# Sliding-window attention and a gated unit on one core: loads by units of four heads, square transposes, and scores issued half a pair ahead

## The chip, the cores and the metric

The kernel runs on one core of a Trainium2 chip. The core has TensorE (PE in the profile; PEld is its weight loads), VectorE (DVE), ScalarE (ACT), GpSimd (POOL) and SyncE (SP), and 16 DMA engines that SP, ACT and POOL hand transfers to. Each engine works through its own instructions in program order and waits on semaphores. The metric is the device time in microseconds, the median of several runs; lower is better.

## What is computed

```python
def _attn_ref(q, k, v):                       # (8, 8, 576, 64) each, float32
    window, dilation, scale = 32, 4, 1.0 / np.sqrt(D)
    scores = scale * np.matmul(q, k.transpose(0, 1, 3, 2))
    rel = pos[:, None] - pos[None, :]
    mask_plain = (rel >= 0) & (rel < window)
    mask_dil = (rel >= 0) & (rel < window * dilation) & (rel % dilation == 0)
    masks = [mask_plain if h < H // 2 else mask_dil for h in range(H)]
    ...                                       # masked softmax over keys
    return np.matmul(attn, v)
def _moe_ref(x, w_val, conv_w, w_out):        # x: heads joined, (8, 576, 512)
    ...                                       # causal, 5 taps per channel
        gate_pre += conv_w[k][None, None, :] * xp[:, k:k + S, :]
    gate = 1.0 / (1.0 + np.exp(-gate_pre))
    return (gate * (x @ w_val)) @ w_out       # (8, 576, 512) float32
```

## The kernel before

The kernel works on 32 pairs of heads (8 batches, 4 pairs each; pairs 0 and 1 are plain, 2 and 3 dilated). The program order of every engine is the order in which the Python code issues; nothing is rescheduled. Positions are split in four residue classes r = position mod 4 with 144 members each; a dilated head is a plain window of 32 inside each class.

*Loads.* `load_qk(i)` and `load_v(i)` fetch one pair, all on SP's queue. A partition takes four neighbouring positions of a head, a row of 1 KB; as 144 partitions do not fit, each tensor comes as a tile of 96 (`qa`, `ka`, `va`) and one of 48 rows (`qzd`/`kzd` for dilated, `qzp`/`kzp` for plain pairs; `vz` has 80). Plain v comes in rows of 256 bytes (`vp`), in six overlapping chunks of 128 keys. `convert(i)` casts on POOL: v of dilated pairs (L136), q and k of plain pairs (L143). Pair i+2 is loaded and cast while pair i runs.

*Attention of a pair.* `transpose_in` turns q and k to head-dimension-major with TensorE (L161 and L163 for dilated, L167 and L171 for plain pairs), in transposes of 96 and 48 rows; DVE copies the result out (L182), ACT for k of plain pairs (L179). `scores(i, hf)`, hf being a half of the pair, multiplies k by q for two heads side by side, 64 rows of the array each (L197), into one of two score tiles `sc` in PSUM; exp on ACT (L212) and the mask on DVE (L219) give `et`. Dilated classes are cut in 96 and 48 queries. `attn_v(i, hf)` multiplies `et` with v (L236, L240 dilated, L246 plain), writes into the same score tile, and DVE divides by the sum (reciprocal L251, product into `xn` L256). `transpose_x` turns `xn` back (L269, L271 by turns for dilated; L275 plain), and ACT copies it into `xT` (L278).

*Gated unit.* It works on groups of 512 tokens (the last ones of 448, 320 and 256). For each of four channel blocks there is a unit C (conv as five diagonal matmuls, L303, tanh on ACT, L307) and a unit V (product with w_val, L315, gating on DVE into `y_all`, L320); for each 128 tokens a unit O (product with w_out, L329, copy out on ACT, L332, output DMA from ACT's queue, L333). These units, the transposes and the copies share four PSUM banks (`bank`). Units of a batch become available when its four pairs are done. They wait in a queue, and `fill(share)` issues units as long as a budget lasts, so that they lie between the steps of the attention:

```python
    per = 3.2
    for i in range(n_steps):
        ...                        # load_qk, load_v, convert of pair i + 2
        scores(i, 0)
        scores(i, 1)
        fill(per * 0.35)
        attn_v(i, 0)
        if i + 1 < n_steps:
            transpose_in(i + 1, "q")
            transpose_in(i + 1, "k")
        attn_v(i, 1)
        fill(per * 0.65)
        transpose_x(i)
```

What is left in the queue after the last pair is issued at the end.

## Time and profile before

| | |
|---|---|
| median of three runs | 228.96 us (226.93 to 231.23) |
| the profiled execution | 225.51 us, of which the span of the profile is 223.8 us |
| mean granted TensorE clock | 0.992 |
| DMA | 41.82 MB in 58757 packets, mean 187 GB/s |

The page's first part has the busy time of each engine, its share of the span and its instructions; the second cuts the span into 40 slices of 5.6 us, a digit being a busy share in tenths:

```profile
PE 189.1 (85%) x2279; PEld 127.0 (57%) x2292; DVE 128.4 (57%) x311; ACT 108.7 (49%) x190; POOL 65.0 (29%) x123
...
PE   2666689878988898898898898889888988999992
...
DVE  2566664775667556663666659656776566532320
ACT  2234444356554655475544753465536654643442
...
DMA  5799999747779799869989779778986300221232
GB/s 144 240 220 207 236 216 225 211 120 232 213 212 231 234 254 224 217 222 258 233 192 243 234 217 237 181 244 227 232 213 212 118 3 0 99 91 47 100 141 94
```

And some of its groups (line, engine, operation, output and input, shape, count, then busy us, mean ns of one, and the idle time before them):

```profile
L256 DVE TENSOR_TENSOR xn<-sc,rec 96x512 bf16<-96x512 f32 (+1 forms) x64 | 39.7, 620 | 2.2
L212 ACT ACTIVATE et<-sc 128x576 bf16<-128x576 f32 x64 | 38.5, 660 | 4.8 <-PE sc L197 4.8
L332 ACT ACTIVATE osb<-bank 128x512 f32<-128x512 f32 x36 | 21.6, 601 | 29.4 <-PE bank L329 23.4
L179 ACT COPY kT<-bank 128x576 bf16<-128x576 bf16 x16 | 10.2, 638 | 20.4 <-PE bank L171 16.4
L182 DVE COPY qT<-bank 128x576 bf16<-128x576 bf16 x32 | 14.2, 444 | 3.3 <-PE bank L163 3.0
```

A busy TensorE is not one at its peak: the end of a matmul is modelled, and an isolated one of 65 columns counts some 200 ns.

### The profile page before, as it was taken

Reading aid. Unit: us, or ns where it says so; the run is one execution under the profiler, and the core shown is the slowest. Engines: PE = TensorE matmul, PEld = TensorE weight load, DVE = VectorE, ACT = ScalarE, POOL = GpSimd, SP = SyncE. Lnnn points to the kernel's source line nnn. Section 1 sums busy time; section 2 is a strip of 40 time slices with the busy share of each in tenths; the row PEclk is TensorE's granted clock in tenths of the full one; section 3 lists DMA queues with packets and bytes.
Section 4 is the critical chain, followed back from the end, with each engine's and each line's share of the span. In section 5 each row is a group of like instructions: output and inputs, shape, how many; then the busy total and the mean of one; then the engine's idle time right before and its main releaser. Section 6 shows DMA issues by size and latency. Waiting matters only on the chain.

```text
span 223.8 us, 5850 instructions
## 1 busy us (share of the span) xinstructions
PE 189.1 (85%) x2279; PEld 127.0 (57%) x2292; DVE 128.4 (57%) x311; ACT 108.7 (49%) x190; POOL 65.0 (29%) x123
## 2 busy tenths in 40 slices
PE   2666689878988898898898898889888988999992
PEld 0544545545655576556775686558655666454670
DVE  2566664775667556663666659656776566532320
ACT  2234444356554655475544753465536654643442
POOL 4296506420516150524146024602360200000000
PEclk9999999999999999996999999999999999999999
DMA  5799999747779799869989779778986300221232
GB/s 144 240 220 207 236 216 225 211 120 232 213 212 231 234 254 224 217 222 258 233 192 243 234 217 237 181 244 227 232 213 212 118 3 0 99 91 47 100 141 94
DMA packets 58757, 41.82 MB, mean 187 GB/s; under 512 B 29029, under 2 KB 54117, under 8 KB 58730
## 3 DMA queue, kind: packets, MB, share of 16 engines
q1 hardware_dynamic: 52480, 30.95, 56.1%
q10 hardware_dynamic: 5194, 9.45, 11.8%
q0 software_dynamic: 1056, 1.05, 2.9%
q8 instruction: 18, 0.29, 0.6%
q14 instruction: 9, 0.07, 0.1%
HBM read 33.04 MB, written 9.44 MB: 190 GB/s over the span
## 4 chain that ended last, share of the span: by engine, by line
PE 45%; DMA 15%; ACT 13%; DVE 10%; issue 7%; SPq 6%; ACTq 2%; POOL 0%; DVEq 0%
PE bank L303 16%; ACT et L212 9%; PE bank L315 8%; PE bank L329 5%; DVE et L219 4%; ACT osb L332 4%; DMA qa<-in_q_dram 4%; DVE xn L256 4%; DMA vp<-in_v_dram 3%; PE bank L269 3%; PE sc L246 2%; PE bank L271 2%; DMA ka<-in_k_dram 2%; ACTq L333 2%; DMA kzd<-in_k_dram 2%
## 5 line engine op out<-in xcount | busy, mean ns | idle before, releaser
L303 PE MATMUL bank<-xT,conv_diag 128*128 128x320 bf16 (+7 forms) x319 | 46.3, 295 | 0.3 <-DMA kzd<-in_k_dram 0.3
L256 DVE TENSOR_TENSOR xn<-sc,rec 96x512 bf16<-96x512 f32 (+1 forms) x64 | 39.7, 620 | 2.2
L212 ACT ACTIVATE et<-sc 128x576 bf16<-128x576 f32 x64 | 38.5, 660 | 4.8 <-PE sc L197 4.8
L307 ACT ACTIVATE gate<-bank 128x512 bf16<-128x512 f32 (+3 forms) x40 | 22.0, 556 | 32.8 <-PE bank L303 32.8
L315 PE MATMUL bank<-xT,w_val_b 128*128 128x320 bf16 (+7 forms) x254 | 37.1, 285 | 0.3 <-issue 0.3
L136 POOL CAST vda<-va 96x512 bf16<-96x512 f32 x16 | 10.0, 622 | 92.9 <-DMA va<-in_v_dram 79.3
L332 ACT ACTIVATE osb<-bank 128x512 f32<-128x512 f32 x36 | 21.6, 601 | 29.4 <-PE bank L329 23.4
L320 DVE SCALAR_TENSOR_TENSOR y_all<-gate,bank 128x512 bf16<-128x512 bf16 (+3 forms) x40 | 25.1, 628 | 18.0 <-PE bank L315 9.1
L303 PEld LDWEIGHTS <-conv_diag 128*128 128x128 bf16 x320 | 27.8, 100 | 12.6 <-issue 1.4
L329 PE MATMUL bank<-w_out_b,y_all 128*128 128x512 bf16 x134 | 33.7, 380 | 0.8 <-DVE y_all L320 0.2
L219 DVE TENSOR_TENSOR et<-et,mask_d 128x576 bf16<-128x576 bf16 x32 | 16.7, 524 | 27.9 <-ACT et L212 26.9
L278 ACT COPY xT<-bank 128x576 bf16<-128x576 bf16 x32 | 20.4, 637 | 23.1 <-PE bank L271 17.8
L219 DVE TENSOR_TENSOR et<-et,mask_p 128x576 bf16<-128x576 bf16 x32 | 16.8, 532 | 25.6 <-ACT et L212 24.6
L315 PEld LDWEIGHTS <-w_val_b 128*128 128x128 bf16 x256 | 20.8, 97 | 8.1
L329 PEld LDWEIGHTS <-y_all 128*128 128x128 bf16 x144 | 12.8, 98 | 14.4 <-DVE y_all L320 1.8
L179 ACT COPY kT<-bank 128x576 bf16<-128x576 bf16 x16 | 10.2, 638 | 20.4 <-PE bank L171 16.4
L236 PE MATMUL sc<-vda,et 96*128 96x65 bf16 x128 | 12.2, 203 | 7.6 <-DVE et L219 3.7
L246 PE MATMUL sc<-vp,et 128*128 128x65 bf16 x192 | 12.1, 201 | 7.5 <-DVE et L219 4.2
L269 PE MATMUL bank<-ident_b,xn 96*128 96x96 bf16 x64 | 14.1, 221 | 4.4 <-DVE xn L256 4.4
L251 DVE RECIPROCAL rec<-sc 96x8 f32<-96x8 f32 (+1 forms) x64 | 12.2, 191 | 9.5 <-PE sc L246 7.7
L182 DVE COPY qT<-bank 128x576 bf16<-128x576 bf16 x32 | 14.2, 444 | 3.3 <-PE bank L163 3.0
L236 PEld LDWEIGHTS <-et 96*128 96x128 bf16 x128 | 8.1, 100 | 14.1 <-DVE et L219 13.6
(62 smaller groups left out, 243.5 us busy)
## 6 DMA issues: line engine op xcount, KB each, us to landing
out_dram<-osb ACTq DMA_DIRECT2D x36, 256.0 KB, 2.3
qa<-in_q_dram SPq DMA_DIRECT2D x32, 192.0 KB, 4.1
ka<-in_k_dram SPq DMA_DIRECT2D x32, 192.0 KB, 3.4
vp<-in_v_dram SPq DMA_DIRECT2D x32, 160.0 KB, 3.8
va<-in_v_dram SPq DMA_DIRECT2D x16, 192.0 KB, 3.6
vz<-in_v_dram SPq DMA_DIRECT2D x16, 160.0 KB, 3.8
qzd<-in_q_dram SPq DMA_DIRECT2D x32, 48.0 KB, 3.4
kzd<-in_k_dram SPq DMA_DIRECT2D x32, 48.0 KB, 3.1
```

The lines of the kernel that those rows point to most:

```text
L212: nc.scalar.activation(out=et[:, :, 0:HALF], in_=ps[:, :, 0:HALF], func=AF.Exp, scale=scale)
L219: nc.vector.tensor_tensor(out=ev, in0=ev, in1=for_mask, op=ALU.mult)
L236: nc.tensor.matmul(out=ps[:, x, hh * DA:(hh + 1) * DA], lhsT=et[0:96, x, hh * 96:hh * 96 + 128], rhs=c0[:, hh, r, :], start=True, stop=True)
L256: nc.vector.tensor_tensor(out=xo, in0=av[:, :, :, 0:D], in1=rec[:, :, 0:n, None].to_broadcast([96, 2, n, D]), op=ALU.mult)
L269: nc.tensor.transpose(out=pv[:, r, 0:96], in_=xn[:, 2 * r, :, :].rearrange("p h d -> p (h d)"), identity=ident_b[0:96, 0:96])
L278: nc.scalar.copy(out=xT[:, g, c0:c0 + S].rearrange("p (t r) -> p t r", r=R), in_=pv.rearrange("p r t -> p t r"))
L303: nc.tensor.matmul(out=ps[:, o:o + ln], lhsT=conv_diag[:, c, kk, :], rhs=xT[:, c, s:s + ln], start=(kk == 0), stop=(kk == K - 1))
L307: nc.scalar.activation(out=gate[:, 0:n], in_=ps[:, 0:n], func=AF.Tanh, scale=0.5)
L315: nc.tensor.matmul(out=ps[:, o:o + ln], lhsT=w_val_b[:, mc, c * 128:(c + 1) * 128], rhs=xT[:, mc, col:col + ln], start=(mc == 0), stop=(mc ...
L320: nc.vector.scalar_tensor_tensor(out=y_all[:, c, t0:t0 + n], in0=gate[:, 0:n], scalar=1.0, in1=ps[:, 0:n], op0=ALU.add, op1=ALU.mult)
L329: nc.tensor.matmul(out=ps[0:n, :], lhsT=y_all[:, c, t0:t0 + n], rhs=w_out_b[:, c, :], start=(c == 0), stop=(c == NCH - 1))
L332: nc.scalar.activation(out=osb[0:n, :], in_=ps[0:n, :], func=AF.Copy, scale=0.5)
```

## The change

Work is now loaded and transposed by units of two pairs (four heads): for every batch the dilated unit, then the plain one.

- Loads: q and k of a unit fill 128 partitions. A partition takes 36 neighbouring positions (9.2 KB) in a dilated unit, with q in partitions 0 to 63 and k in 64 to 127 of one tile, and 9 positions (2.3 KB) in a plain one. SP issues one half, ACT the other. v of a dilated unit comes in tiles of 128 and 48 rows, v of a plain unit in one transfer. Buffers: two units of each kind rather than four pairs.
- Transposes into q and k: 18 of 128x128 per unit (two parts of eight, one of two). DVE copies all q, ACT all k; the copies spread the columns with a step of 9.
- Dilated classes are cut in 128 and 16 queries rather than 96 and 48. The transposes back of a dilated pair are four of 128 rows, then four of 16.
- The loop runs over half-pairs: the scores of half-step j+2 are issued in half-step j, the mask of j+1 behind the product of j, the transposes back one half-step later.
- The fill spreads the units of all groups but the last two evenly over the half-steps from 9 on. Groups end in 384, 384 and 256 tokens. `y_all` becomes three rotating tiles.

```diff
-    def load_qk(i):
...
+    def load_unit(u):
+        b, d = units[u]
+        hs = slice(4 * d, 4 * d + 4)
+        t = {}
+        if d:
+            t["qk"] = inbuf.tile([128, JD * D], FP32, name="qkd")
+            for n, (src, eng) in enumerate(((q, nc.sync), (k, nc.scalar))):
+                eng.dma_start(out=t["qk"][64 * n:64 * n + 64],
+                              in_=src[b, hs].rearrange("h (p j) d -> (h p) (j d)", j=JD))
...
+            nc.sync.dma_start(out=t["va"], in_=rows[0:128])
+            nc.sync.dma_start(out=t["vz"][W:80], in_=rows[96:TT])
+        else:
+            for name, src in (("q", q), ("k", k)):
+                t[name] = inbuf.tile([128, 2, JP * D], FP32, name=f"{name}p")
+                for e, eng in enumerate((nc.sync, nc.scalar)):
+                    eng.dma_start(
+                        out=t[name][64 * e:64 * e + 64],
+                        in_=src[b, 2 * e:2 * e + 2].rearrange("h (p j) d -> p h (j d)", j=JP))
...
+    def convert_qk(u):
+        t = loaded[u]
+        for name in ("k", "q"):
+            c = work.tile([128, JP, 2, D], BF16, name=f"{name}c", bufs=2)
+            nc.gpsimd.tensor_copy(
+                c.rearrange("p j h d -> p h j d"),
+                t[name].rearrange("p h (j d) -> p h j d", j=JP))
...
+    def transpose_in(u, part):
...
+        engines = ((qT, nc.vector.tensor_copy), (kT, nc.scalar.copy))
...
+                for m in range(8):
+                    nc.tensor.transpose(out=ps[:, m * 128:(m + 1) * 128],
+                                        in_=cols(2 * m + part), identity=ident_b)
+                for n, (dst, copy) in enumerate(engines):
+                    copy(out=dst[:, part * S:(part + 1) * S].rearrange(
+                             "p (a m) -> p a m", m=9)[:, :, 0:8],
+                         in_=ps.rearrange("p (m n a) -> p n a m", m=8, n=2)[:, n])
...
+                for j in range(8):
+                    nc.tensor.transpose(out=ps[:, j * 128:(j + 1) * 128],
+                                        in_=flat(c[:, j]), identity=ident_b)
+                copy(out=dst.rearrange("p (a j) -> p a j", j=JP)[:, :, 0:8],
+                     in_=ps.rearrange("p (j a) -> p a j", j=8))
...
     def scores(i, hf):
...
-                mm(hh * 96, 96, kT[:, o:o + 128], qT[:, o:o + 96])
...
-                mm(192 + hh * 48, 48, kT[:, o + 64:o + 192], qT[:, o + 96:o + TT])
...
+                mm(hh * 128, 128, W + o, o)
...
+                mm(256 + hh * X1, X1, W + o + 64, o + 128)
...
+    def masks(i, hf):
...
+        nc.vector.tensor_tensor(out=ev, in0=ev, in1=m, op=ALU.mult)
...
             for r in range(R):
-                nc.tensor.transpose(out=pv[:, r, 0:96], in_=xn[:, 2 * r, :, :].rearrange("p h d -> p (h d)"),
-                                    identity=ident_b[0:96, 0:96])
-                nc.tensor.transpose(out=pv[:, r, 96:TT], in_=xn[0:48, 2 * r + 1, :, :].rearrange("p h d -> p (h d)"),
-                                    identity=ident_b[0:48, 0:48])
+                nc.tensor.transpose(out=pv[:, r, 0:128], in_=flat(xn[:, 2 * r]),
+                                    identity=ident_b)
+            for r in range(R):
+                nc.tensor.transpose(out=pv[:, r, 128:TT], in_=flat(xn[0:X1, 2 * r + 1]),
+                                    identity=ident_b[0:X1, 0:X1])
...
-    for i in range(n_steps):
...
+    for part in range(3):
+        transpose_in(0, part)
+    scores(0, 0)
+    scores(0, 1)
+    masks(0, 0)
+    for j in range(2 * n_steps):
+        i, hf = j // 2, j % 2
+        u, e = i // 2, i % 2
+        if hf == 0 and e == 0:
+            if u + 2 < len(units):
+                load_unit(u + 2)
+        if hf == 0:
+            if i + 2 < n_steps and is_dil(i + 2):
+                convert_v(i + 2)
+            if e == 0 and u + 1 < len(units) and not units[u + 1][1]:
+                convert_qk(u + 1)
...
+        share = max(0.0, left[0]) / max(1, left[1]) if j >= first_fill else 0.0
...
+        attn_v(i, hf)
+        if j + 1 < 2 * n_steps:
+            masks((j + 1) // 2, (j + 1) % 2)
+        if hf == 0 and i > 0:
+            transpose_x(i - 1)
+        if u + 1 < len(units):
+            if (e, hf) == (0, 0):
+                transpose_in(u + 1, 0)
+            elif (e, hf) == (0, 1):
+                transpose_in(u + 1, 1)
+                transpose_in(u + 1, 2)
+        fill(share * 0.6)
+        if hf == 0 and i > 0 and i % NG == 0:
+            queue.extend(ready_after.get(order[i - 1][0], []))
+        if j + 2 < 2 * n_steps:
+            scores((j + 2) // 2, (j + 2) % 2)
+        fill(share * 0.4)
...
+    transpose_x(n_steps - 1)
+    queue.extend(ready_after[B - 1])
     while queue:
         run_item()
```

## The prediction, made before the run

> **What bounds the kernel now.** I read the slices of the page first (PE at 8 to 9 tenths from 32 us on, nine at the end, DMA at 7 to 9 until 180 us), then cut the span at two places that the timeline shows: the first conv matmul (31.96 us) and the last copy into xT (198.33 us). The view of windows, whose columns are stretch, length, busy time of each engine with its instructions, granted clock, DMA share and GB/s:
>
> ```profile
> core 0: us, PE busy (x) PEld busy (x) DVE busy (x) ACT busy (x) POOL busy (x), PEclk, DMA share, GB/s
> 0.00:32.00 32.00, 18.65 (x229) 13.28 (x231) 18.61 (x62) 10.69 (x18) 16.20 (x43) 1.00 0.98 209
> 32.00:198.30 166.30, 149.56 (x1925) 101.45 (x1934) 103.70 (x237) 88.46 (x154) 48.84 (x80) 0.99 0.74 199
> 198.30:223.80 25.50, 20.92 (x127) 12.25 (x130) 6.12 (x12) 9.51 (x19) 0.00 (x0) 1.00 0.23 84
> ```
>
> The first stretch is the DMA engines' (share 0.98); the middle one is TensorE's (150 of 166 us, the next engine 104); the last is the rest of the gated unit on TensorE. What TensorE waits for in the middle, from the waits of 32 to 199 us (total, times, longest):
>
> ```profile
> PEld L236 <- DVE et L219: 11.1, 16, 1.2
> PEld L246 <- DVE et L219: 7.4, 8, 1.4
> PEld L269 <- DVE xn L256: 4.1, 6, 0.7
> PEld L275 <- DVE xn L256: 3.2, 7, 0.6
> PEld L303 <- issue: 1.4, 5, 0.3
> PEld L271 <- issue: 1.1, 5, 0.3
> ```
>
> These are 28.3 us: 18.5 for masked scores, 7.3 for normalized x, 2.5 of issue. DMA is not among them. The timeline shows how such a wait arises, and a second loss that counts as busy:
>
> ```profile
> 180.20 0.44 PE L197 MATMUL sc<-qT,kT 64*128 64x96 bf16 x16
> ...
> 181.06 1.21 ACT L212 ACTIVATE et<-sc 128x576 bf16<-128x576 f32 x2
> 181.76 1.00 DVE L219 TENSOR_TENSOR et<-et,mask_d 128x576 bf16<-128x576 bf16 x2 [1.59 <-ACT et L212]
> 182.28 0.11 PEld L236 LDWEIGHTS <-et 96*128 96x128 bf16 x2 [0.83 <-DVE et L219]
> ...
> 182.51 0.21 PEld L167 LDWEIGHTS <-qca 96*128 96x128 bf16 x4
> ...
> 183.28 0.16 PEld L171 LDWEIGHTS <-kcz 48*128 48x128 bf16 x4
> ...
> 183.48 0.11 PEld L236 LDWEIGHTS <-et 96*128 96x128 bf16 x2
> ...
> 185.66 0.10 PEld L269 LDWEIGHTS <-xn 96*128 96x128 bf16 x1
> ...
> 186.68 0.30 PEld L197 LDWEIGHTS <-kT 64*128 64x128 bf16 x12
> ```
>
> Scores at 180.20, exp and mask behind them, and only one val unit in between: attn_v waits. Then 16 transposes of 96 and 48 rows by turns last 182.51 to 183.48, 0.97 us; the 12 of a dilated pair in the same view (177.15 to 177.65), as many columns, last 0.50. The eight of L269/L271, 96 and 48 rows by turns, last 185.66 to 186.68, 1.02. So a change of row count between those two costs (0.97-0.50)/4 = 0.12 or (1.02-8x0.042)/7 = 0.10 us; I use 0.11.
>
> **The sum of before.** In the chain a conv unit of 512 tokens takes 1.10 us ("L303 x10"), a val unit 0.87 ("L315 x8"), an out unit 0.9 (half of "L329 x8", 1.89, less the last one's tail). A group is 4 of each, 11.5 us; nine groups 103.5. The tail holds 20.6 of it (198.2 to 218.85), so the middle has 82.9. The middle is 166.3 = 28.3 waits + 82.9 + 55.1, and 55.1 is attention: 28 pairs at 1.97 us of TensorE.
>
> **The change part by part.**
>
> *Matmul order.* Transposes into q and k: 36 of 128 columns per batch for 56 of 96 and 48, the same 4608 columns, so their streaming time stays; the four row changes of each plain pair go: 0.47 x 16 = 7.5 us. The dilated transposes back go from seven changes to two (four of 128 rows, four of 16, out again): 5 x 0.11 x 16 = 8.8. Against that, scores (64 rows) are visited twice in a pair, not once: 0.22 per visit; today a plain pair pays 0.22 and a dilated one 0.11, as 48 to 64 rows goes without a gap (186.67 to 186.68). Extra: 16 x (0.22+0.33) = 8.8. Net 7.5 us, 0.23 per pair, bounds 0 and 0.4: attention becomes 1.74. The 16-row transposes have no row in this trace; nearest is 48 rows, so they get the same 0.11 in and out. [...]
>
> *Half-pair pipeline.* Scores of half-step j+2 are issued in half-step j, mask j+1 behind xn j, and the transpose back a half-step later. The 18.5 and 7.3 us of waits go: exp 0.66, mask 0.53 lie under more than a half-step of about 2.8 us. What is late next: scores j+2 write the score bank that xn j must have read. From attn_v j that is 0.1 + 0.19 (L251) + 0.62 (L256) = 0.9 us, or 1.6 if a y (0.68) stands ahead on DVE. TensorE has 0.6 of the fill, 0.97 us, plus transposes: about 1.9, 1.5, 1.5, 0.97 us in the four half-steps of two pairs. Wait 0 to 0.63 in the last, little in the others; I take 0.22 in the mean, 55 half-steps, 12.1 us, and keep 2.5 of issue: 14.6. Bounds 2.5 (nothing waits) and 28.3 (as today). Behind the waiting scores stand the other 0.4 of the fill and the next attn_v.
>
> *Fill.* It now spreads 3968 tokens over half-steps 9 to 63 and leaves 640. TensorE does the same units; only the place moves. Tail: 1.25 x 11.5 = 14.4 for 640 tokens, 1.2 ahead (last transposes 0.4, xT 0.64), 5.0 behind the last matmul as now (218.85 to 223.8): 20.6. Middle: 103.5-14.4 = 89.1.
>
> *Copies.* The k copies of all pairs are ACT's. ACT takes 382 ns for 256 columns (L307) and 599 for 512, so 0.27 for 128, 1.03 for 1024: dilated 2x0.60+0.27, plain 1.03+0.27, times 8 is 22.2 us for 10.2 (L179). q on DVE is strided. By its f32 rows (L256, 553 ns for 384, 686 for 512) it is 0.69, 0.29, 1.22: 25.5 us; by the packed row (L182, 444 ns for 576) 14.2; now 21.3. [...] Either way DVE stays near 130 us, 2.1 per half-step, under TensorE's 2.5. POOL: 16 casts of 1152 columns replace 64 of 512 (41 us); at 1.25 ns a column (637/512) 23 us. Hidden.
>
> *Loads.* 31 MB as before (8 x 3.87), but q and k in rows of 9.2 or 2.3 KB rather than 1 KB. From the queues' lines,
>
> ```profile
> q1 hardware_dynamic: 52480, 30.95, 56.1%
> q10 hardware_dynamic: 5194, 9.45, 11.8%
> ```
>
> an engine moves 30.95/(0.561x16x223.8) = 15.4 GB/s in small rows and 22.4 in the output's 2 KB rows. SP has 49 issues instead of 240; ACT gets 24, at 0.34 to 0.45 us each. A batch needs 3.87 + 1.18 MB in 22 us, 230 GB/s; slices of the page reach 258.
>
> *Start.* The first MoE work waits for nine half-steps. DVE does about today's 18.6 us plus one half-step (1.4), from 8 us on (two pairs must have landed, 1.2 MB): not under 28. Units 0 to 2, q and k of unit 3 and one weight, 8.1 MB, at 220 GB/s (8 to 32 us today) would take to 38. I take 33, near today's 32, where the two ends meet.
>
> **The sum.** Start 33.0. Middle 27.5 x 1.74 + 89.1 + 14.6 = 151.6 (2.76 per half-step). Tail 20.6. Span 205.2 against 223.8; with 1.7 outside it as now (225.51) 206.9. The median of the runs is 228.96, 1.5% over the profiled one: 210.
>
> **The rivals.**
> 1. *The waits only move* (the bank wait, or ACT late with banks, as large as 28.3): middle 165.3, span 218.9, 224 us by the same steps. For: today's four banks and two score buffers stay. Against: TensorE's cover counted above.
> 2. *DMA sets the pace.* For: share over 1.0 and 220 GB/s in the start. At 220 a batch takes 23.0 us, 6.9 batches 158, start 38: 216.6 span, 222 us. Against: 170 to 193 us, where loads had all but ended (share 0.20), took 23.0 us a batch, against 22.6 to 24.2 before, so DMA does not hold the middle today; and longer rows.
> 3. *ACT's queue blocks* (slower). ACT has 120.8 us of work, 12.2 of output issues, 8.6 of load issues: 141.6, less some 14 in the start and 9.5 in the tail about 118 in a middle of 152, a slack of 2.5 us per two pairs (four half-steps). These two pairs hold 1.5 load issues on ACT, each behind a wait for an earlier transfer's semaphore, with exp, gates and k copies queued behind, and TensorE behind these. Free up to 1.7 us each; at 2.8 it adds 1.65 x 13.75 = 23 us, and the kernel is slower than before; at 3.6 (median landing today) 39 us, near 250. For: SP waits 11.1 and 10.9 us for outputs to land. Against: ACT's own waits for a DMA sum to 2 us today.
> 4. *It does not do what it says:* strided copies or casts come late and transposes wait for them; the price is that of rival 1.
>
> **How the numbers follow.** The forecast has 0.70, with its own range 199 to 220 (start 28 to 38, waits 5 to 22 us). Rival 2 has 0.11, rivals 1 and 4 together 0.09, rival 3 0.10. The range goes to 226, past rivals 1 and 2, and leaves out rival 3 and some 0.08 below 199. The border is 2%, 224.4 and 233.5, about what runs between 226.9 and 231.2 can tell from no change. Faster: 0.70, most of rival 2, a third of 1 and 4; slower: rival 3 and a little.
>
> **What would show it.** Right: waits of attn_v for et near zero; transposes back of a dilated pair in 0.6 us, not 1.02; a tail from the last xT copy of about 20 us; half-steps of 2.7 to 2.8 us; first conv matmul at 29 to 37 us. Wrong: ACT rows whose idle time a DMA ended (rival 3), DMA share near 1 from 40 to 170 us with transposes waiting for qkd or kc (rival 2), or waits of score matmuls for xn over 22 us (rival 1).

## The result and the profile after

The changed kernel is slower: 249.55 us (median of four runs, 246.08 to 251.74) against 228.40 us for the kernel before, measured beside it, a ratio of 1.090 with a 95% interval of 1.074 to 1.106. The ratios and intervals leave out the longest executions where these had a lower granted clock, of the changed kernel the one of 251.74 us at 0.917 (the other three: 246.08 to 249.73 us at 0.935 to 0.943). The prediction said 210 us, and rival 3, its only case for "slower", had 0.10.

The same three windows as in the prediction, now of the changed kernel: up to the first weights of a conv unit, up to the last copy into xT, and the rest (columns: stretch, length, busy time of each engine with its instructions, granted clock, DMA share, GB/s):

```profile
core 0: us, PE busy (x) PEld busy (x) DVE busy (x) ACT busy (x) POOL busy (x), PEclk, DMA share, GB/s
0.00:47.90 47.90, 20.82 (x257) 16.93 (x258) 24.08 (x70) 16.56 (x26) 17.31 (x43) 1.00 1.08 224
47.90:229.80 181.90, 157.71 (x1802) 104.03 (x1801) 108.64 (x227) 102.89 (x176) 28.09 (x36) 0.92 0.68 163
229.80:247.70 17.90, 13.74 (x113) 8.88 (x111) 3.90 (x8) 6.02 (x13) 0.00 (x0) 0.98 0.22 83
```

Against the forecast of 33.0, 151.6 and 20.6 us, the start is 14.9 us too long and the middle 30.3; only the tail does what was said. Two columns tell where to look. In the start the DMA share is over 1 at 224 GB/s for 48 us, although the rows are longer (the clock of 1.00 shown there has no clock record behind it, see experiment 5). In the middle the clock is 0.92, where before it was 0.99, and the DMA engines have time left. The slices of the page show that the low clock comes in spots:

```profile
PE   0328274798999959996989589986999399899993
...
PEclk9999999999999997999799859996899869999999
```

The dips lie four slices apart, some 25 us, which is one batch. Each stands beside or just behind a slice with less TensorE work. Cutting one of them out in windows of the same view, same columns:

```profile
134.10:137.50 3.40, 3.12 (x30) 1.55 (x28) 2.54 (x6) 1.80 (x4) 1.75 (x2) 1.00 0.06 16
137.50:140.90 3.40, 1.71 (x20) 0.76 (x17) 0.85 (x3) 2.28 (x4) 1.61 (x3) 1.00 0.40 157
140.90:147.80 6.90, 5.06 (x53) 4.09 (x54) 2.07 (x5) 4.01 (x7) 0.00 (x0) 0.52 1.00 257
```

TensorE is busy for half of the 3.4 us before 140.9, and then runs 6.8 us at half clock. In all, the middle has 27.3 us at half clock, in stretches of 3.4 and 6.8 us, from 93, 117, 141, 168 and 196 us on; that is 13.7 us of full clock lost. The kernel before has one such stretch of 3.4 us in its middle.

What happens in that half-idle window is in the timeline of the same stretch:

```profile
138.53 0.32 PE L211 MATMUL sc<-qT,kT 64*128 64x128 bf16 x8
138.87 0.65 ACT L225 ACTIVATE et<-sc 128x576 bf16<-128x576 f32 x1 [0.71 <-PE sc L211]
...
139.55 0.46 DVE L236 TENSOR_TENSOR et<-et,mask_p 128x576 bf16<-128x576 bf16 x1 [2.56 <-ACT et L225]
...
140.07 0.37 PE L263 MATMUL sc<-vp,et 128*128 128x65 bf16 x6 [1.22 <-ACT xT L299]
...
141.31 0.40 PE L211 MATMUL sc<-qT,kT 64*128 64x128 bf16 x4 [0.88 <-DVE xn L274]
```

There is not one unit of the gated unit between scores and attn_v, nor between attn_v and the next scores. The fill has nothing left, and the waits that it should cover lie bare: 1.22 and 0.88 us. (The view puts the 1.22 us down to a copy into xT. What attn_v needs is the mask, which ended at 140.01 us, 0.06 us before it began.)

A third thing shows in ACT's groups of the page (busy and mean ns of one, then the idle time before them and what ended it):

```profile
L172 ACT COPY kT<-bank 128x512 bf16<-128x512 bf16 x16 | 9.4, 589 | 23.2 <-DVE qT L172 23.2
...
L196 ACT COPY kT<-bank 128x128 bf16<-128x128 bf16 x8 | 5.8, 722 | 22.3 <-DVE qT L196 22.3
```

ACT stands idle for 45.5 us until DVE has copied q. Both engines copy out of one bank here, q and k having been transposed together, and the program lets ACT read the bank only when DVE has. Where q and k have a bank each (L189), no copy waits for the other engine: ACT's idle time before these copies is 9.9 us, all of it for TensorE. Behind a waiting k copy stand exp and the gates, in ACT's order.

### The profile page after: what moved, and what is told of

Read it like the earlier page. It is cut to its first block, busy times and chain, and to the rows that moved or that the text cites. A ratio compares the mean times of both kernels' runs of the same rounds, so it can differ in the third digit from the quotient of the medians.

```text
span 247.7 us, 5286 instructions
## 1 busy us (share of the span) xinstructions
PE 192.3 (78%) x2168; PEld 129.8 (52%) x2168; DVE 136.6 (55%) x304; ACT 125.5 (51%) x214; POOL 45.4 (18%) x79
## 3 DMA queue, kind: packets, MB, share of 16 engines
q0 software_dynamic: 1056, 1.05, 2.5%
## 4 chain that ended last, share of the span: by engine, by line
PE 43%; DVE 21%; DMA 14%; ACT 12%; issue 3%; POOL 3%; ACTq 3%; SPq 0%; POOLq 0%; DVEq 0%
PE bank L324 14%; DMA kp<-in_k_dram 9%; PE bank L336 9%; DVE xn L274 6%; PE bank L353 5%; DMA vz<-in_v_dram 5%; ACT osb L356 4%; PE sc L211 4%; DVE et L236 3%; DVE qT L189 3%; PE bank L187 3%; ACT et L225 3%; ACTq L357 2%; DVE y L343 2%; ACT kT L196 2%
## 5 line engine op out<-in xcount | busy, mean ns | idle before, releaser
L324 PE MATMUL bank<-xT,conv_diag 128*128 128x384 bf16 (+7 forms) x340 | 51.8, 302 | 2.9 <-ACT kT L196 1.9
L225 ACT ACTIVATE et<-sc 128x576 bf16<-128x576 f32 x64 | 42.6, 671 | 15.7 <-PE sc L211 11.5
L274 DVE TENSOR_TENSOR xn<-sc,rec 128x512 bf16<-128x512 f32 (+1 forms) x64 | 39.8, 622 | 2.2
L343 DVE SCALAR_TENSOR_TENSOR y<-gate,bank 128x512 bf16<-128x512 bf16 (+2 forms) x40 | 26.3, 657 | 25.2 <-PE bank L336 19.5
L269 DVE RECIPROCAL rec<-sc 128x8 f32<-128x8 f32 (+1 forms) x64 | 12.5, 196 | 49.0 <-PE sc L257 34.5
L353 PE MATMUL bank<-w_out_b,y 128*128 128x512 bf16 x144 | 36.6, 380 | 2.5 <-DVE y L343 1.1
L336 PE MATMUL bank<-xT,w_val_b 128*128 128x320 bf16 (+7 forms) x272 | 37.6, 279 | 0.5 <-ACT kT L196 0.4
L324 PEld LDWEIGHTS <-conv_diag 128*128 128x128 bf16 x340 | 29.6, 105 | 14.9 <-issue 5.3
L211 PE MATMUL sc<-qT,kT 64*128 64x128 bf16 (+1 forms) x448 | 21.7, 215 | 15.4 <-DVE xn L274 13.1
L328 ACT ACTIVATE gate<-bank 128x512 bf16<-128x512 f32 (+2 forms) x40 | 24.1, 608 | 18.2 <-PE bank L324 17.3
L211 PEld LDWEIGHTS <-kT 64*128 64x128 bf16 x448 | 14.0, 103 | 33.0 <-DVE xn L274 13.9
L353 PEld LDWEIGHTS <-y 128*128 128x128 bf16 x144 | 12.4, 97 | 16.2 <-DVE y L343 4.1
L252 PE MATMUL sc<-vda,et 128*128 128x65 bf16 x128 | 13.3, 213 | 7.3 <-DVE et L236 4.2
## 6 DMA issues: line engine op xcount, KB each, us to landing
va<-in_v_dram SPq DMA_DIRECT2D x8, 512.0 KB, 12.1
```

The source lines that it names most:

```text
L211: nc.tensor.matmul(out=ps[:, x, out_c:out_c + ln], lhsT=kw[rb, k0:k0 + 128], rhs=qT[rb, q0:q0 + ln], start=True, stop=True)
L225: nc.scalar.activation(out=et[:, :, 0:HALF], in_=ps[:, :, 0:HALF], func=AF.Exp, scale=scale)
L252: nc.tensor.matmul(out=ps[:, x, hh * DA:(hh + 1) * DA], lhsT=et[:, x, hh * 128:hh * 128 + 128], rhs=c0[:, hh, r, :], start=True, stop=True)
L269: nc.vector.reciprocal(out=rec[0:m, :, 0:n], in_=av[:, :, :, D])
L274: nc.vector.tensor_tensor(out=xo, in0=av[:, :, :, 0:D], in1=rec[0:m, :, 0:n, None].to_broadcast([m, 2, n, D]), op=ALU.mult)
L324: nc.tensor.matmul(out=ps[:, o:o + ln], lhsT=conv_diag[:, c, kk, :], rhs=xT[:, c, s:s + ln], start=(kk == 0), stop=(kk == K - 1))
```

## The experiments

The stages of every run, from its profile (start: to the first weights of a conv unit; middle: to the end of the last copy into xT). The ratio of experiments 1 to 14 is to the kernel before on the chip of the experiment, which had medians of 228.1 to 229.7 us. The stages are those of one execution each, in experiment 4 one of 235.54 us, in the row "before" one of 225.51 us.

| kernel | median us | ratio (95%) | start | middle | clock in it | tail |
|---|---|---|---|---|---|---|
| before | 228.96 | | 31.6 | 167.4 | 0.990 | 24.8 |
| changed | 249.55 | 1.090 (1.074 to 1.106) | 47.8 | 181.9 | 0.925 | 18.0 |
| 1 one engine per bank | 246.06 | 1.079 (1.070 to 1.088) | 44.4 | 183.4 | 0.909 | 17.9 |
| 2 SP issues all loads | 247.33 | 1.085 (1.075 to 1.096) | 44.1 | 184.1 | 0.937 | 17.9 |
| 3 both of these | 239.41 | 1.049 (1.040 to 1.058) | 42.6 | 177.6 | 0.942 | 17.8 |
| 4 before, with the pipeline alone | 234.54 | none | 38.5 | 178.9 | 0.933 | 16.5 |
| 5 changed, paced fill | 232.37 | 1.015 (1.009 to 1.022) | 47.7 | 163.6 | 0.992 | 18.2 |
| 6 = 3 with paced fill | 221.76 | 0.972 (0.965 to 0.979) | 42.5 | 158.7 | 0.994 | 18.2 |
| 7 = 4 with paced fill | 222.99 | 0.975 (0.968 to 0.981) | 38.7 | 165.7 | 1.000 | 16.7 |
| 10 = 6, loads of full width | 228.36 | 1.002 (0.997 to 1.007) | 38.9 | 170.0 | 0.970 | 18.4 |
| 11 = 6, short casts | 220.95 | 0.961 (0.949 to 0.974) | 41.8 | 159.4 | 0.990 | 18.0 |
| 12 = 10, short casts | 218.49 | 0.954 (0.946 to 0.963) | 38.4 | 160.1 | 0.993 | 18.1 |
| 13 = 11, masks first | 220.21 | 0.965 (0.962 to 0.969) | 41.7 | 159.0 | 0.991 | 18.4 |
| 14 = 12, masks first | 216.85 | 0.950 (0.947 to 0.954) | 37.6 | 159.8 | 1.000 | 18.0 |

### 1 to 3: the copies of one bank, and the loads on ACT's queue

Theory A: ACT's k copy waits for DVE's q copy of the same bank, and exp waits behind it. Theory B: the halves that ACT issues stand behind ACT's own work, so k lands late. Theory C, the rival: the slower clock and the extra changes between 128 and 64 rows. Experiment 1 lets one engine take both copies out of a bank, the engines by turns (the comment stands here for the same edit at the ninth columns):

```diff
-                for n, (dst, copy) in enumerate(engines):
+                for n, dst in enumerate((qT, kT)):
+                    copy = engines[part][1]          # ninth columns: engines[(u // 2) % 2][1]
```

> The changed kernel, but the two copies out of one transpose bank (q and k) go to one engine: dilated part 0 to DVE, part 1 to ACT, the ninth columns to both by turns. The work per engine stays. Theory A (ACT's k copy waits for DVE's q copy of the same bank, 45.5 us of ACT idle, and exp stands behind it in ACT's order): those waits go, the waits of attn_v for et fall from 12 us in the middle to under 5, and the time falls by 12 to 25 us from 249.6. Theory B (the halves of the loads that ACT issues come late and hold the start and the transposes): first conv matmul stays near 48 us, time falls by under 6 us. Theory C (more changes between 128 and 64 rows and a lower clock): nothing, within 4 us.

Experiment 2 issues all loads from SP:

```diff
-            for n, (src, eng) in enumerate(((q, nc.sync), (k, nc.scalar))):
+            for n, (src, eng) in enumerate(((q, nc.sync), (k, nc.sync))):
...
-                for e, eng in enumerate((nc.sync, nc.scalar)):
+                for e, eng in enumerate((nc.sync, nc.sync)):
```

> The changed kernel, but all loads are issued by SP, none by ACT. Theory B: the first conv matmul comes at 33 to 40 us rather than 47.9, no cast of kc waits 10 us for kp, the time falls by 8 to 14 us. Theory A: the start may move, the middle does not, under 8 us in all. Theory C: within 4 us. If the DMA engines' rate of 224 GB/s in the start is what holds it, whoever issues, the first conv matmul stays at 45 us or more.

Experiment 3 makes both edits:

> The changed kernel with both edits: copies out of a bank on one engine, all loads from SP. A and B both true: 249.6 less 20 to 35 us, so 215 to 230, near or below the kernel before. If C holds the middle: still over 240.

By the medians each edit alone was worth 2 to 3.5 us, which the intervals do not tell from nothing (1.070 to 1.088 and 1.075 to 1.096, against 1.074 to 1.106); both together were worth 10, and the kernel stayed slower than before. Neither A nor B met the forecast for its own experiment. A had given 12 to 25 us, and under 5 us of waits of attn_v for et: experiment 1 has 3.5 us, and 16.0 us of these waits. B had given a start of 33 to 40 us: experiment 2 has 44.1. For both together they had given 215 to 230 us. C's forecast, within 4 us, held for 1 and 2, but not for 3, where it was over 240. In experiment 1 no k copy waits for DVE any more: these 45.5 us of waiting went, and the middle did not get shorter (183.4 for 181.9), so by itself this waiting did not hold it. The two edits together show 5.2 us of start and 4.3 of middle; that late halves and late copies cover for each other when only one is mended is a reading of this, which no run shows by itself. The low clock stayed in all three.

### 4: the pipeline alone

The kernel before, with its own loads (issued three pairs ahead), transposes and copies, with the half-pair loop and the even fill:

```diff
+    for j in range(2 * n_steps):
+        i, hf = j // 2, j % 2
...
+        attn_v(i, hf)
+        if j + 1 < 2 * n_steps:
+            masks((j + 1) // 2, (j + 1) % 2)
...
+        fill(share * 0.6)
...
+        if j + 2 < 2 * n_steps:
+            scores((j + 2) // 2, (j + 2) % 2)
+        fill(share * 0.4)
```

> The kernel before with the half-pair pipeline and the even fill alone (its own loads, one pair further ahead, its own transposes and copies). If the pipeline does what the prediction said of it, the waits of attn_v and of the transposes back (25.8 us in the middle) go and the scores' wait for xn stays under 12 us: 210 to 221 us. If the pipeline is the cause of the loss (theory C: twice as many visits to 64 rows, a clock of 0.94), it is slower than before: 230 to 245 us.

234.54 us: its runs of 229.28, 233.53, 235.54 and 236.84 us lie too far apart for a ratio. The shortest, at a clock of 0.975, is not told from the kernel before on that chip (226.14 to 231.79); the other three have clocks of 0.949 to 0.956, and the profiled one 0.93 in its middle. None comes near the 210 to 221 us that the prediction's pipeline would give. So the gain is missing, and the low clock there, without the new loads or copies, which A and B do not explain. The median lies where C put it, but C does not say where the low clock comes from. That led to theory D.

### 5 to 7: a fill that runs dry

Theory D comes from working the planner through by hand, with its costs of 1.05 for C and 0.9 for V and O. It spreads the work of 3968 tokens evenly over 55 half-steps, about 1.6 each. But each of batches 0 to 5 releases one group, worth 11.4, and that queue is empty in less than the eight half-steps until the next release. Batch 3 issues 1.05, 1.95, 1.95, 1.05, 1.8, 1.8, 1.8, 0; every batch from 2 to 5 ends with a 0, batch 6 with two, and batch 7 gets 2 to 3.6 in each half-step. The edit divides what lies in the queue by the half-steps left until the next release (batch 3: 1.8, 2.1, 0.9, 1.05, 1.95, 0.9, 1.8, 0.9):

```diff
-        share = max(0.0, left[0]) / max(1, left[1]) if j >= first_fill else 0.0
+        to_go = min(8 - (j - 1) % 8, 2 * n_steps - j)
+        share = sum(COST[x[0]] for x in queue) / to_go if j >= first_fill else 0.0
```

> The changed kernel with one edit: the share of a half-step is the cost that now lies in the queue, divided by the half-steps left until the next batch releases work, so that the last half-steps of a batch keep something to do (in a replay of the planner by hand 0.9 to 2.1 per half-step, none with zero, where the changed kernel has one or two zeros per batch). Theory D (the even share empties the queue before each release, TensorE then streams too little for one 3.4 us window and the clock is halved in the next one or two): granted clock of the span from 0.94 to above 0.98, the halved windows after 90 us go, 236 to 242 us. Theory A/B/E alone (copies wait, late halves, a start bound by the transfers): the dry half-steps are only the place where those waits show, the time stays at 247 to 251 us and the clock below 0.95.

> The same edit on the kernel with both copies of a bank on one engine and all loads issued by SP (239.4 us). Theory D: its four or five halved windows go, 227 to 233 us, clock above 0.98. If the copies' order and the pacing compete for the same idle time: 235 to 240 us.

> The same edit on the kernel before with the half-pair pipeline alone (234.5 us, its undisturbed run 229.3). Theory D: 219 to 226 us, faster than the kernel before, with a clock above 0.98; the pipeline itself was then right and the fill's plan wrong. Rival: the pipeline's own wait of the scores for the softmax result (11.5 us in the run of the pipeline alone) sets the pace, 228 to 235 us.

All three come out on D's side, 7 within its range and 5 and 6 below theirs: 17.2 us less for the changed kernel (232.37 for 249.55), 17.7 for the kernel with both edits, 11.6 for the pipeline alone (6.3 against the shortest of its runs). Kernel 7 answers C too: it visits 64 rows as often as experiment 4, with a clock of 1.00 in the middle. The middle of the changed kernel, same view as above, with the edit:

```profile
47.70:211.30 163.60, 146.97 (x1786) 96.05 (x1801) 109.24 (x227) 102.39 (x176) 28.61 (x36) 0.99 0.72 180
```

The same work takes 163.6 us instead of 181.9. TensorE is busy 10.7 us less, since after the first 2.7 us nothing in it runs at half clock, and idle 7.6 us less, since no half-step is bare. The expectation had the clock of the whole span rise; it did not (0.944), because this execution is recorded with 23.9 us at half clock in the start, where TensorE waits for data anyway. The windows by stage are what decides, and in the start not even they: the changed kernel's trace has clock records only from 49.0 us on, and the view shows 1.00 before. The same transposes of 128 columns show it, in the changed kernel (0 to 47.9 us, then 48 to 93 us) and in this run (26.5 to 47.7 us, recorded at half clock):

```profile
L187 PE MATMUL bank<-ident_b,qc 128*128 128x128 bf16 x16 | 2.1, 310 | 0.0
L187 PE MATMUL bank<-ident_b,qc 128*128 128x128 bf16 x8 | 0.6, 218 | 0.0
L187 PE MATMUL bank<-ident_b,qc 128*128 128x128 bf16 x8 | 1.0, 310 | 0.0
```

The 310 ns of the changed kernel's start are those of recorded half clock, not the 218 of later, so I take its start to have run at the lower clock as well.

The busy share alone does not say which window leads to half clock. Two windows and the ones behind them, of experiment 4 and of kernel 6:

```profile
80.40:83.80 3.40, 2.57 (x44) 1.84 (x43) 2.74 (x7) 2.05 (x4) 1.19 (x3) 1.00 0.60 217
83.80:87.20 3.40, 3.40 (x35) 2.35 (x35) 0.76 (x3) 1.62 (x3) 0.61 (x1) 0.50 0.84 215
...
133.00:136.40 3.40, 2.02 (x32) 1.62 (x32) 2.56 (x5) 1.75 (x4) 1.87 (x4) 1.00 0.88 232
136.40:139.80 3.40, 3.40 (x48) 2.79 (x47) 2.41 (x6) 1.82 (x4) 0.70 (x1) 1.00 1.12 209
```

TensorE was busy for 2.57 us before the half clock, and 2.02 us did not bring it. What counts in place of the busy share is not settled here.

Kernels 6 and 7 beat the changed kernel and also the one before, the latter by 2.8 and 2.5%. They differ in loads, transposes, the cut of the queries and copies. In the middle TensorE is busy 144.8 us in 6 and 158.7 in 7: the new transposes and the new cut save 13.9 us of it, of which the time shows 7.0 (158.7 for 165.7).

### 8 and 9: the rate of the loads by itself

Theory E: a transfer into 64 partitions is slow, so the start is bound by the loads. Both kernels only load, in phases of which each begins when the one before has landed; no part of the reference is computed. The two calls that matter (phases a and c of the first kernel; `half_rows` puts the 64 rows at 0 or 64, here at 0):

```python
nc.sync.dma_start(out=big[n][0:64], in_=q[n, 0:4].rearrange("h (p j) d -> (h p) (j d)", j=36))
nc.sync.dma_start(out=big[n][:, 0:18 * D], in_=k[n, 0:4].rearrange("h (p j) d -> (h p) (j d)", j=18))
```

> Leaves out all computation: six phases of loads from SP alone, each 2.36 MB and each begun when the one before has landed: (a) 64 partitions with rows of 9216 bytes, always the lower half; (b) the same, lower and upper half by turns; (c) 128 partitions with rows of 4608 bytes; (d) 64 partitions with two rows of 2304 bytes each, lower and upper half by turns, as in the changed kernel; (e) 96 and 48 partitions with rows of 1 KB, as in the kernel before; (f) 128 partitions with rows of 256 bytes. [...] Rival (the queue or the row's length sets the rate, the partitions do not): c like a, and e slower than both.

One window in each phase, a to f in order (length, busy DVE and POOL, clock, DMA share, GB/s):

```profile
5.50:14.50 9.00, 4.12 (x3) 0.00 (x0) 1.00 1.03 213
19.50:28.50 9.00, 0.00 (x0) 0.00 (x0) 1.00 1.03 228
32.50:38.00 5.50, 0.00 (x0) 0.00 (x0) 1.00 0.96 380
43.50:51.50 8.00, 0.00 (x0) 0.00 (x0) 1.00 1.03 232
57.00:63.50 6.50, 0.00 (x0) 0.00 (x0) 1.00 1.09 235
69.00:77.00 8.00, 0.00 (x0) 0.00 (x0) 1.00 1.30 224
```

The DMA engines are full in all six, but 64 partitions give 213 to 232 GB/s with rows of 9216 and of 2304 bytes alike, and 128 partitions 380. The kernel before's rows of 1 KB give 235: the longer rows of the change win nothing. Very short rows do cost: those of 256 bytes, over 128 partitions, get 224 (the last line).

A second kernel of loads asks whether the number of partitions or their place sets this rate:

> Leaves out all computation, as the run with loads alone: six phases, each 2.36 MB (the fourth and the third part by rows as said) and begun when the one before has landed. (a) rows of 9216 bytes, q into partitions 0 to 63 from SP and k into 64 to 127 from ACT at the same time, twice the bytes (4.72 MB); (b) 128 partitions with rows of 2304 bytes; (c) 96 partitions with rows of 1 KB, 3.15 MB; (d) 128 partitions with rows of 1 KB, 4.19 MB; (e) partitions 0 to 31 with rows of 9216 bytes; (f) partitions 32 to 95 with rows of 9216 bytes. [...] a: 390 GB/s if two halves in two queues fill each other's gaps, 220 GB/s if an engine gives its time to the two in turn. Rival (the number of rows of a transfer sets the rate, wherever they lie): f 220 GB/s like the lower half, e slower than 150 GB/s; a second rival (length of the row): b and d below 300 GB/s.

The second kernel, phases a to d and f:

```profile
6.00:24.00 18.00, 3.96 (x2) 0.00 (x0) 1.00 1.01 236
29.50:38.00 8.50, 0.00 (x0) 0.00 (x0) 1.00 1.02 366
44.00:52.00 8.00, 0.00 (x0) 0.00 (x0) 1.00 1.11 250
57.00:66.00 9.00, 0.00 (x0) 0.00 (x0) 1.00 1.06 350
91.50:97.50 6.00, 0.00 (x0) 0.00 (x0) 1.00 0.95 333
```

Two halves loaded at once from two queues, as the changed kernel does it, stay at 236. Rows of 2304 bytes into 128 partitions reach 366, rows of 1 KB 350, but 250 when only 96 partitions are written. And 64 partitions are no bar if they are 32 to 95: 333 GB/s. So in these two kernels it is the place that counts (64 rows of 9216 bytes: 213 into 0 to 63, 333 into 32 to 95), not the number of rows and, from 1 KB on, hardly their length (350, 366 and 380 into 128 partitions). Why the place sets the rate, no run shows. Each phase ran once. Phase e is not read, since its two transfers wrote the same rows and waited for each other.

### 10 to 12: full-width loads, and what they collided with

Experiment 10 gives kernel 6 loads over 128 partitions (rows of 4608 and 2304 bytes):

```diff
-                eng.dma_start(out=t["qk"][64 * n:64 * n + 64],
-                              in_=src[b, hs].rearrange("h (p j) d -> (h p) (j d)", j=JD))
+                eng.dma_start(out=t["qk"][:, 18 * D * n:18 * D * n + 18 * D],
+                              in_=src[b, hs].rearrange("h (p j) d -> (h p) (j d)", j=18))
```

> The kernel with both copies of a bank on one engine, all loads from SP and the paced fill (221.8 us), with the same number of loads of q and k, the same bytes, but each over all 128 partitions (rows of 4608 and 2304 bytes). The heads and positions of q and k come to other places, so the output is another; instructions and shapes are the same. Theory E (the transfers into 64 partitions set the start): first conv weights at 33 to 36 us in place of 42.5, 212 to 216 us. Rival F (DVE with 16 diagonal weights and POOL with the masks hold the start, DVE being 86% busy between 28 and 42.5 us): start 40 to 43 us, 219 to 222 us.

The loads moved 278 GB/s in the start, where kernel 6 had 203 to 234, and the start became 3.6 us shorter, not 6.5 to 9.5 as E had it, and not under 2.5 as F had it. But the kernel came out 6.6 us slower, with a middle of 170.0 us. One group had grown, the mask of dilated pairs: 15.5 us in kernel 6, here

```profile
L239 DVE TENSOR_TENSOR et<-et,mask_d 128x576 bf16<-128x576 bf16 x32 | 25.7, 804 | 3.7 <-ACT et L228 3.5
```

Five of the 32 masks took 1.7 to 2.85 us, the shortest 0.44. All five begin beside POOL's casts and end 0.3 us after the last of them. The timeline beside one:

```profile
60.15 0.61 POOL L136 CAST vdb<-vz 80x512 bf16<-80x512 f32 x1
60.41 2.85 DVE L239 TENSOR_TENSOR et<-et,mask_d 128x576 bf16<-128x576 bf16 x1
...
60.71 1.15 POOL L143 CAST kc<-kp 128x1152 bf16<-128x1152 f32 x1
...
61.80 1.15 POOL L143 CAST qc<-qp 128x1152 bf16<-128x1152 f32 x1
...
63.30 0.11 PEld L255 LDWEIGHTS <-et 128*128 128x128 bf16 x2 [1.68 <-DVE et L239]
```

The mask begins beside one cast on POOL, outlasts the two that follow without a gap, and ends 0.3 us after the last; attn_v waits for it. In kernel 6, k lands later, and the casts mostly miss the masks (4 of all 64 take over 0.85 us, not the six that the expectation below counts). This is theory G: faster loads let POOL's casts follow one another without a gap, and a mask of DVE that meets them stands until they are done. To test it, the casts are cut in three, each of three positions, in kernel 6 (experiment 11) and in kernel 10 (experiment 12):

```diff
-            nc.gpsimd.tensor_copy(
-                c.rearrange("p j h d -> p h j d"),
-                t[name].rearrange("p h (j d) -> p h j d", j=JP))
+            for j in range(0, JP, 3):
+                nc.gpsimd.tensor_copy(
+                    c[:, j:j + 3].rearrange("p j h d -> p h j d"),
+                    t[name][:, :, j * D:(j + 3) * D].rearrange("p h (j d) -> p h j d", j=3))
```

> The kernel with one engine per bank, all loads from SP and the paced fill (221.8 us), with each of POOL's casts of kc and qc cut into three of three positions. Theory G (a mask of VectorE that starts beside POOL's casts stands until they are done; here six of the masks took 0.85 to 1.31 us in place of 0.45): those masks shorter than 0.9 us, the time 0 to 2 us shorter, 219 to 222 us. Rival H (POOL takes time by the instruction, so three small casts are longer than one and kc comes later): 223 to 226 us.

> The same edit on the kernel with q and k loaded over all 128 partitions (228.4 us; heads and positions of q and k lie elsewhere). There five masks took 1.7 to 2.85 us: each began beside the casts of kc and qc and ended where they ended. Theory G: the masks stay under 1.2 us, the middle goes from 170 back to 157 to 161 us, since the three halved clock windows that follow these masks go as well, and the time is 212 to 218 us. Rival I (the earlier loads move other waits, and the long masks only happen to lie beside the casts): the masks stay long or the time stays at 225 to 229 us.

With short casts the masks of kernel 12 take

```profile
L240 DVE TENSOR_TENSOR et<-et,mask_d 128x576 bf16<-128x576 bf16 x32 | 16.9, 527 | 4.3 <-ACT et L229 4.2
```

8.8 us less; the three halved clock stretches that had followed three of the long masks are gone too, and the time falls from 228.36 to 218.49 us. In kernel 11, where the casts rarely met the masks, the edit changes next to nothing (220.95 for 221.76, intervals of the ratios overlap). That is G against rival I. Two of G's figures were missed: the longest mask takes 1.48 us, not under 1.2, and 218.49 us is just over its 218. Nor does a mask always stand to the end: this longest one is done 0.37 us before the last of the four casts beside it. By the medians full-width loads are then worth 2.5 us (218.49 for 220.95), though the intervals overlap: the start is 3.4 us shorter, the middle 0.7 longer. Why a cast on POOL holds up a mask on DVE, no run shows.

### 13 and 14: the rest of the start

POOL makes mask_p between its casts of v and its first cast of k. The edit moves these eight instructions ahead of the first cast of v, in kernels 11 and 12:

```diff
+    nc.gpsimd.memset(mask_p, 1.0)
+    band(mask_p[:, 1, 0:96], W, [[1, 96]], 1, W)
...
     convert_v(0)

     load_unit(1)
...
-    nc.gpsimd.memset(mask_p, 1.0)
-    band(mask_p[:, 1, 0:96], W, [[1, 96]], 1, W)
```

> The kernel with one engine per bank, SP loads, paced fill and short casts (220.95 us, start 41.8), with POOL's eight instructions that make mask_p moved ahead of its first cast of v. Until then POOL has nothing to do before the first v has landed; so far these instructions stand between v's casts and the first cast of k, 2.7 us. Theory J (the order of POOL's queue is part of the late start): first conv weights 2 to 3 us earlier, 39 to 40 us, and 218 to 219 us. Rival E (the transfers alone set this start at 222 GB/s): k has not landed earlier, start 41 to 42.5, 220 to 222 us.

> The same move in the kernel with q and k over all 128 partitions and short casts (218.5 us, start 38.4; heads and positions of q and k lie elsewhere), where k has landed when POOL comes to it. Theory J: start 35 to 36.5 us, 215 to 217 us. Rival: DVE, 23 us busy in a start of 38, takes the place of POOL and the start stays above 37.5 us.

With narrow loads nothing moves (start 41.7 for 41.8): the first cast of k comes no earlier (16.7 us for 16.2) and waits for the transfer, so the transfers hold that start. With full-width loads it comes 2.4 us earlier (12.6 for 15.0), but the start only goes from 38.4 to 37.6, where the rival had it (above 37.5), and the time from 218.49 to 216.85 us (the intervals of the ratios overlap). That DVE holds the rest, as the rival says, was not tested. The fastest kernels that compute the reference are those with narrow loads: 11 and 13, 0.961 (0.949 to 0.974) and 0.965 (0.962 to 0.969) of the time before, and 6 with 0.972 (0.965 to 0.979), not told apart by their intervals. A layout that loads full width and still brings the heads to their places was not written.

## Why the prediction was wrong

*Fill, "only the place moves": the step that failed most.* It was costed at nothing because TensorE does the same units, and the same work was then counted as cover in the waits term ("TensorE has 0.6 of the fill, 0.97 us"), as if every half-step got its mean. Where the units lie was never worked through per half-step, though the planner's few lines allow it. The half-steps at the end of batches 2 to 6 get none: the waits lie bare there, and 3.4 or 6.8 us at half clock follow. Experiment 5 prices it at 17.2 us. No rival had it: rival 1 comes nearest, but looked for too few banks and not for missing work.

*Waits, 14.6 us.* By the same accounting (waits of weight loads in the middle) the changed kernel has 47.1 us, kernel 5 has 36.3 and kernel 6 has 32.2, against 28.3 before. The predicted mechanism is there, but is not the whole: scores waiting for xn take 10.3 us in the changed kernel and 16.8 in kernel 6, against the 12.1 predicted. What was missing is attn_v waiting for et: 12.4 us in the changed kernel, 3.5 with the paced fill alone (kernel 5), 1.0 in kernel 6, so most of it came from the dry half-steps. Not all of such a wait is on the path, since TensorE still works off earlier matmuls: TensorE's own waits in the middle are 11.8 us in kernel 6, 16.0 in the kernel before.

*Copies, "hidden".* Mostly so by their busy time: ACT at 102.9 and DVE at 108.6 of 181.9 us. Two sizes were wrong: a ninth column of 128 elements takes 0.72 us on ACT and 0.71 on DVE, not 0.27 and 0.29. The columns go out with a step of 9, and the rows they were sized by are packed; that the step is the reason was not tested. And the sum of busy times did not see that two engines share a bank, 45.5 us of ACT's waiting in order. Experiments 1 to 3 price this and the late loads together: 10.1 us (239.41 for 249.55).

*Loads and start, 33 us.* The step that set 15.4 GB/s "in small rows" against "22.4 in the output's 2 KB rows" put the gain down to the row's length. The output comes from 128 partitions, the loads of before went to 96 and 48; for loads the runs show that the place makes the difference (333 GB/s into partitions 32 to 95, 380 into all 128), and that 64 partitions in one half, 0 to 63 or 64 to 127, stay at 213 to 236 GB/s with rows of 2304 and 9216 bytes. The upper bound of 38 us in the prediction was worked out with this rate and was the better one. Of the 14.8 us between 33 and 47.8, the late halves with the copies are 5.2 (experiment 3), the width of the loads 3.4 (41.8 against 38.4, experiments 11 and 12), POOL's masks 0.8 (experiment 14), and the paced fill, the short casts and the differences between executions 0.8. These are steps between single profiles. What holds the last 4.6, from 37.6 to 33, was not settled.

*Rival 3, ACT blocked by load issues*, was the only case on the right side, with the wrong mechanism: ACT waits for DVE, and a DMA ended only 0.9 us of its idle time. Right side by luck, then. Its neighbour, halves that land late because ACT issues them, shows in the start alone (44.1 us for 47.8 in experiment 2). *Rival 2, DMA sets the pace*, holds for the start only: in the middle the share is 0.68. *Rival 1*'s sign, scores waiting for xn over 22 us, did not come either (10.3).

*What was right.* The tail, nearly: 18 us for 20.6. The order of the matmuls: the transposes back of a dilated pair take 0.57 us from 99.31 to 99.88, where 0.6 was predicted and 1.02 stood before:

```profile
99.31 0.39 PE L288 MATMUL bank<-ident_b,xn 128*128 128x128 bf16 x4
...
99.63 0.25 PE L291 MATMUL bank<-ident_b,xn 16*128 16x16 bf16 x4
```

The term of 7.5 us was too small for TensorE's busy time, 13.9 us (kernels 7 and 6), and about right for the time, 7.0; as kernels 6 and 7 differ in loads and copies too, the second may be chance. The pipeline: with a fill that does not run dry it takes the kernel before from 228.1 to 223.0 us without the new loads and transposes.

The sum, then: 249.6 less 17.2 (fill) less 10.6 (copies and loads) is 221.8, kernel 6. From there to the forecast's 210 it is 11.8 us, in the spans 14.1 (219.3 against 205.2): the start has 9.5 of these and the middle 7.1, and the tail gives 2.4 back. The 7.1 are the rest of two larger errors: by the prediction's accounting kernel 6 has 17.6 us more of waits in the middle (32.2 for 14.6) and 10.5 less of work (126.5 for 137.0).

## What to carry to other kernels

When work is moved about to cover waits, replay its planner step by step and look at the step that gets least, not at the mean: releases come in lumps, and here a TensorE left half idle for one window of 3.4 us paid again at half clock. Before calling a copy hidden, look at what it shares with its neighbours, here a bank with another engine's copy (45.5 us of waiting), and before counting on an instruction's time, at what runs beside it, here a mask of 0.45 us that took 2.85 beside POOL's casts; neither is in the busy times of before. Price a load by which partitions one transfer covers (213 GB/s into 0 to 63, 380 into all 128) before counting the bytes of its rows.

## What the runs showed of the hardware

- A window of 3.4 us in which TensorE was busy for 1.71 us was followed by 6.8 us at half clock; in the changed kernel such stretches came five times, one batch apart, twice for 3.4 and three times for 6.8 us, 27.3 us in all. In experiment 4 a window with 2.57 us busy led to it, in kernel 6 one with 2.02 did not.
- Transposes of 128 columns took 310 ns in the start of the changed kernel, where the view shows a clock of 1.00, and 218 ns later; at recorded half clock (experiment 5) they took 310.
- Partitions 32 to 95 take 333 GB/s (experiment 9), 0 to 63 take 213 (experiment 8), both with 64 rows of 9216 bytes; rows of 1 KB into 96 partitions get 250 GB/s and into 128 get 350 (experiment 9).
- A masked product of 0.45 us on DVE took 2.85 us beside three casts in a row on POOL (experiment 10), and at most 1.48 us once two of them were cut in three (experiment 12).
- Removing 45.5 us of waiting from ACT made the middle no shorter (183.4 us for 181.9, experiment 1), while faster loads made the kernel 6.6 us slower (228.36 for 221.76, experiment 10).
